# Scores of three pairs laid end to end in shared blocks, and four sequence-closing turns moved from TensorE to DMA

## The chip, the cores and the metric

The kernel runs on one core of one Trainium2 chip. The metric is the device time of one execution in microseconds (us), lower is better. Each run on record carries a state, and one that took over 1.5% longer than the fastest of its kernel is called slow. All runs compared here are in the fast state unless said otherwise. A "ratio" is the mean time of one kernel's fast runs over the mean of the fast runs of the kernel before in the same rounds, so it is not quite the ratio of the medians that are quoted.

## The reference, cut to what matters

Eight sequences of 576 tokens with 8 heads of 64 go through causal attention, with 16 "beacon" keys that every query may see. The result, 4608 tokens by 512, goes through two dense layers with a leaky ReLU between.

```python
k_all = np.concatenate([beacon_k, k], axis=2)          # 16 + 576 keys
scores = scale * np.matmul(q, k_all.transpose(0, 1, 3, 2))
scores = np.where(causal, -1000000000.0, scores)       # beacons are never masked
a = np.exp(scores - scores.max(-1, keepdims=True))
a /= a.sum(-1, keepdims=True) + 1e-09
x = np.matmul(a, v_all)                                # then 4608 x 512
h = x @ w_in                                           # 512 -> 2048
out = np.maximum(0.01 * h, h) @ w_out                  # 2048 -> 512
```

## The kernel before

Heads are worked in pairs: 4 pairs a sequence, 32 in all, numbered 0 to 31. The two heads of a pair stand on SBUF partitions 0 to 63 and 64 to 127, so the two score matmuls use the two halves of TensorE's rows at the same time: in the profile of before a block with 976 columns for each head takes 0.52 us, where 1952 columns one after the other would take 0.82 at the 0.216 us of a feed-forward matmul of 512. Keys are cut into 5 tiles; only queries that may see a tile are computed. Before the change, a pair's scores are four PSUM tiles, computed two at a time. I call the matmuls of scores that stand together in TensorE's order a **block**.

```python
SCORES = [
    [(0, 0, 512, 0)],                            # block 1: 512 + 464 columns
    [(1, 112, 464, 512)],
    [(2, 240, 336, 976), (0, 496, 80, 1312)],    # block 2: 336 + 80 + 208 + 80
    [(3, 368, 208, 1440), (4, 496, 80, 1648)],
]
...
for c, q0, w, col in parts:
    for par in range(2):                         # the two heads, 64 rows each
        ps_ = slice(par * 64, par * 64 + 64)
        nc.tensor.matmul(out=sc[:, par, col - c0 : col - c0 + w],
            lhsT=kT[ps_, c * 128 : (c + 1) * 128], rhs=qT[ps_, q0 : q0 + w], ...)
nc.scalar.activation(out=aT[:, :, c0 : c0 + w], in_=sc[:, :, 0:w], func=AF.Exp, scale=0.125)
```

After the values of a pair (`av`), its result `x_nat` must be turned into `xT` for the first dense layer. Three of four pairs of a sequence are turned by DMA (`x_turn`); the last one is turned on TensorE, because the feed-forward matmuls of that sequence are waiting for it. SP (SyncE) is the engine whose queue issues the DMA turns, the loads of V and the output stores.

```python
def finish(g):
    if g in xs:
        x_transposes(g)          # 5 matmuls on TensorE and a copy on VectorE
    ready[0] = chunks_with(g)    # from here on, groups of these 512 tokens may run
...
if old and (g - 2) % NPAIR < NPAIR - 1:
    x_turn(g - 2)                # two DMA transposes on SP's queue
```

Between the attention parts, TensorE's order is filled with feed-forward groups of four matmuls (`acc`): 16 groups of each layer for each 512 tokens. All orders are fixed by the program, engine by engine. (Two profiles of the changed kernel, after and r_after, show 69 instructions of GpSimd, from 103 to 126 and from 160 to 186 us, in the same order, though it stood idle before a copy of keys in one, 4.73 us, and before a copy of queries in the other, 6.20 us.)

## Time and profile before

| | before |
|---|---|
| time | 349.67 us median of 3 (349.06 to 349.69) |
| span in the profile | 347.5 us |
| TensorE busy | 336.1 us, 97% |
| GpSimd, ScalarE, VectorE busy | 57%, 54%, 26% |
| DMA, share of 16 engines, first two thirds / last quarter | 0.5 to 1.2 / about 0.1 |

The prediction below shows and reads the lines that matter: TensorE is the bound from about 60 us on (busy 19.65 to 19.89 of every 20 us until 340). What it says of SP's queue is about the DMA transposes; the added ones are the turns of pairs 19, 23, 27 and 31. Since TensorE's first 66 us are an opening with its own waits for loads, I use one more figure throughout: **the loop**, from the first instruction after the opening (the two second-layer groups behind the transposes of pair 9's keys) to the end of the last matmul. In the chain of before it is 65.81 to 343.56, which is 277.75 us.

### The profile page before, as it was taken

Reading aid. Unit: us, or ns where it says so; the run is one execution under the profiler, and the core shown is the slowest. Engines: PE = TensorE matmul, PEld = TensorE weight load, DVE = VectorE, ACT = ScalarE, POOL = GpSimd, SP = SyncE. Lnnn points to the kernel's source line nnn. Section 1 sums busy time; section 2 is a strip of 40 time slices with the busy share of each in tenths; the row PEclk is TensorE's granted clock in tenths of the full one; section 3 lists DMA queues with packets and bytes.
Section 4 is the critical chain, followed back from the end, with each engine's and each line's share of the span. In section 5 each row is a group of like instructions: output and inputs, shape, how many; then the busy total and the mean of one; then the engine's idle time right before and its main releaser. Section 6 shows DMA issues by size and latency. Waiting matters only on the chain.

```text
span 347.5 us, 7329 instructions
## 1 busy us (share of the span) xinstructions
PE 336.1 (97%) x2951; PEld 168.6 (49%) x2997; DVE 88.8 (26%) x215; ACT 187.9 (54%) x278; POOL 197.9 (57%) x364
## 2 busy tenths in 40 slices
PE   8998999999999999999999999999999999999995
PEld 7664465444444444544444444444454554444442
DVE  3383255103233113311222123212321231000111
ACT  4875864576535873488337843684368204633300
POOL 4794785489997699749974897679422000000000
PEclk9999999999999999999999999999999999999999
DMA  7989999999689747974796469646110120000021
GB/s 141 194 145 208 192 166 194 205 214 154 170 147 226 163 84 107 213 175 80 110 227 142 78 120 226 135 82 103 66 61 18 34 96 32 0 30 32 30 86 65
DMA packets 95857, 43.02 MB, mean 124 GB/s; under 512 B 79824, under 2 KB 90192, under 8 KB 95824
## 3 DMA queue, kind: packets, MB, share of 16 engines
q1 hardware_dynamic: 83200, 28.87, 37.6%
q0 software_dynamic: 12208, 13.49, 26.1%
q8 instruction: 23, 0.38, 0.5%
q10 hardware_dynamic: 416, 0.20, 0.2%
q14 instruction: 10, 0.08, 0.1%
HBM read 37.22 MB, written 9.44 MB: 134 GB/s over the span
## 4 chain that ended last, share of the span: by engine, by line
PE 86%; DMA 6%; DVE 2%; issue 2%; SPq 2%; ACT 1%; POOL 1%; ACTq 0%
PE acc L401 36%; PE acc L385 35%; PE sc L285 7%; PE av L337 7%; DMA w_in_sb<-in_moe_w_in_dram 3%; DMA v_raw<-in_v_dram 2%; SPq L199 1%; DMA v_raw<-in_k_dram 1%; ACT aT L294 1%; DVE x_nat L347 1%; PE tp L359 1%; PE tp L234 0%; DVE kT L246 0%; POOL aT L304 0%; PE tp L241 0%
## 5 line engine op out<-in xcount | busy, mean ns | idle before, releaser
L294 ACT ACTIVATE aT<-sc 128x1024 bf16<-128x1024 f32 (+3 forms) x128 | 104.8, 871 | 62.3 <-PE sc L285 58.7
L385 PE MATMUL acc<-xT,w_in_sb 128*128 128x512 bf16 x551 | 135.4, 379 | 2.4 <-DMA w_in_sb<-in_moe_w_in_dram 0.8
L401 PE MATMUL acc<-w_out_sb,gT 128*128 128x512 bf16 x555 | 134.5, 379 | 1.5 <-issue 0.6
L392 ACT ACTIVATE gT<-acc 128x512 bf16<-128x512 f32 x144 | 85.3, 604 | 76.2 <-PE acc L385 74.1
L304 POOL TENSOR_SCALAR_AFFINE_SELECT aT<-aT 128x256 bf16<-128x256 bf16 (+2 forms) x160 | 57.8, 390 | 49.7 <-ACT aT L294 46.9
L385 PEld LDWEIGHTS <-w_in_sb 128*128 128x128 bf16 x576 | 52.0, 98 | 62.8 <-issue 6.0
L401 PEld LDWEIGHTS <-gT 128*128 128x128 bf16 x576 | 52.0, 98 | 60.7 <-issue 4.8
L413 DVE COPY osb<-acc 128x512 f32<-128x512 f32 x35 | 24.2, 692 | 93.1 <-PE acc L401 87.7
L337 PEld LDWEIGHTS <-aT 128*128 128x128 bf16 (+1 forms) x960 | 37.2, 98 | 13.6 <-issue 1.1
L346 DVE RECIPROCAL rec<-av 128x6 f32<-128x6 f32 x64 | 11.9, 186 | 114.3 <-PE av L337 114.1
L337 PE MATMUL av<-v_aug,aT 128*128 128x65 bf16 (+1 forms) x960 | 40.3, 194 | 0.1
L285 PE MATMUL sc<-qT,kT 64*128 64x80 bf16 (+4 forms) x384 | 36.2, 283 | 1.7 <-DVE kT L246 0.8
L347 DVE TENSOR_TENSOR x_nat<-av,rec 128x384 bf16<-128x384 f32 x64 | 31.4, 491 | 2.2
L267 POOL COPY qT<-q_turn 128x576 bf16<-128x576 bf16 x22 | 26.2, 1189 | 9.0 <-PE av L337 4.5
L285 PEld LDWEIGHTS <-kT 64*128 64x128 bf16 x384 | 12.2, 94 | 27.4 <-issue 21.0
L267 POOL COPY kT<-k_turn 128x576 bf16<-128x576 bf16 x21 | 24.9, 1186 | 0.7 <-DMA k_turn<-k_nat 0.6
L214 POOL CAST v_aug<-v_raw 128x512 bf16<-128x512 f32 (+1 forms) x39 | 22.6, 613 | 2.4 <-DMA v_raw<-in_v_dram 2.4
L148 POOL DMA_DIRECT2D k_raw<-in_k_dram x31 | 19.1, 617 | 5.6 <-DMA w_out_sb<-in_moe_w_out_dram 5.6
L148 POOL DMA_DIRECT2D q_raw<-in_q_dram x32 | 19.7, 617 | 0.8 <-POOLq L661 0.8
L160 POOL COPY q_nat<-q_raw 128x1152 bf16<-128x1152 bf16 x12 | 13.7, 1141 | 1.8 <-DMA q_raw<-in_q_dram 1.8
L160 POOL COPY k_nat<-k_raw 128x1152 bf16<-128x1152 bf16 x12 | 13.7, 1144 | 0.0
L246 DVE COPY qT<-tp 128x576 bf16<-128x576 bf16 x10 | 7.6, 756 | 19.3 <-PE tp L241 13.3
(43 smaller groups left out, 76.9 us busy)
## 6 DMA issues: line engine op xcount, KB each, us to landing
out_dram<-osb SPq DMA_DIRECT2D x35, 256.0 KB, 2.5
v_raw<-in_v_dram SPq DMA_DIRECT2D x24, 256.0 KB, 6.6
q_raw<-in_q_dram POOLq DMA_DIRECT2D x32, 144.0 KB, 6.2
k_raw<-in_k_dram POOLq DMA_DIRECT2D x31, 144.0 KB, 6.2
w_in_sb<-in_moe_w_in_dram POOLq DMA_DIRECT2D x2, 1024.0 KB, 10.4
w_out_sb<-in_moe_w_out_dram POOLq DMA_DIRECT2D x2, 1024.0 KB, 11.1
v_raw<-in_v_dram SPq DMA_DIRECT2D x8, 224.0 KB, 3.2
v_raw<-in_v_dram SPq DMA_DIRECT2D x8, 160.0 KB, 7.3
```

Of the source, the lines that this page charges most:

```text
L148: loaded["qk", g, which] = nc.gpsimd.dma_start(out=raw_of(b, grp)[which][rows], in_=(q, k)[which][b, 2 * hp : 2 * hp + 2].rearrange("h (p ...
L160: copy(out=dst[rows], in_=src[rows].rearrange("p h i d -> p i h d"))
L267: copy(out=operand(g, which).rearrange("c (p i) -> c p i", i=RI), in_=turned[b, grp][which][:, :, e].rearrange("c i p -> c p i"),)
L285: nc.tensor.matmul(out=sc[:, par, col - c0 : col - c0 + w], lhsT=kT[ps_, c * 128 : (c + 1) * 128], rhs=qT[ps_, q0 : q0 + w], start=True, s ...
L294: nc.scalar.activation(out=aT[:, :, c0 : c0 + w], in_=sc[:, :, 0:w], func=AF.Exp, scale=0.125)
L304: nc.gpsimd.affine_select(out=view, in_=view, compare_op=ALU.is_ge, fill=0.0, base=128 - n if lo == 0 else 0, channel_multiplier=-1, patte ...
L337: nc.tensor.matmul(out=avv[:, n, 0 : D + 1], lhsT=aT[0 : ROWS[c], par, a0 : a0 + 128], rhs=va[0 : ROWS[c], c, 2 * hp + par, :], start=(c = ...
L347: nc.vector.tensor_tensor(out=x_nat[:, t0:t1].rearrange("p t e d -> p (t e) d"), in0=avv[:, :, 0:D], in1=rec[:, n0:n1, None].to_broadcast( ...
L385: nc.tensor.matmul(out=acc, lhsT=w_in_sb[:, j, fc * 128 : (fc + 1) * 128], rhs=xT[:, j, i * 512 : (i + 1) * 512], start=(j == 0), stop=(j ...
L392: nc.scalar.activation(out=gT[i][:, fc, :], in_=acc, func=AF.Prelu, alpha=0.01)
L401: nc.tensor.matmul(out=acc, lhsT=gT[i][:, fc, t * 128 : (t + 1) * 128], rhs=w_out_sb[:, fc, :], start=(fc == 0), stop=(fc == NF - 1),)
L413: nc.vector.tensor_copy(out=osb, in_=acc)
```

## The change

The intent is to take work out of TensorE's order. From pair 14 on, the scores of a pair are one strip of 1664 columns (576 + 464 + 336 + 208 + 80). Three strips are cut together into ten PSUM tiles of up to 512 columns, and the ten tiles are issued as five blocks of two, not six blocks of four pieces. The last pairs of sequences 4 to 7 (pairs 19, 23, 27 and 31) are turned by DMA like the others. Both need a new way to place the feed-forward groups: a list of timed events, with the groups spread evenly between the ends of sequences and three of them (`KEPT`) held back as cover behind each end. Loads of queries and keys move with the events.

```diff
+    LAID = 14
+    FLAT = [0, 576, 1040, 1376, 1584, 1664]
...
+    def stretch(parts):
+        sc = ps_sc.tile([128, 2, 512], FP32, name="sc", tag="sc")
+        at = 0
+        for g, lo, hi in parts:
+            for c in range(NKB):
+                a, b = max(lo, FLAT[c]), min(hi, FLAT[c + 1])
+                ...                              # one matmul a head for each piece
+        for g, lo, hi in parts:
+            nc.scalar.activation(out=probs[g][:, :, lo:hi], in_=sc[:, :, at : at + hi - lo], func=AF.Exp, scale=0.125)
+            ...                                  # and the masks of the finished tiles
...
-            if old and (g - 2) % NPAIR < NPAIR - 1:
-                x_turn(g - 2)
+        CUTS = [(0, 512, 1024, 1536, 1664), (0, 384, 896, 1376, 1664), (0, 224, 736, 1248, 1664)]
+        BLOCKS = [((0, 0),), ((0, 1),)], [((0, 2),), ((0, 3), (1, 0))], [((1, 1),), ((1, 2),)], [((1, 3), (2, 0)), ((2, 1),)], [((2, 2),), ((2, 3),)]
+        ONPE = (11, 15)
...
+            if g not in ONPE:
+                events.append((g + 2.63, 5, x_turn, (g,)))
+            if g >= LAID and (g - LAID) % 3 == 0:
+                for i in range(5):
+                    events.append((g + 0.01 + 0.6 * i, 2, block, (g, i)))
...
+                    events.append((4 * b + 1.1, 6, run, ("t%d.0" % (b + 1),)))   # turn of the next sequence's q and k
...
+        KEPT = 3
+            todo = 2 * NF * ready[0] - KEPT - d0
+            aim = d0 + todo * (at - ends[w]) / (ends[w + 1] - ends[w])
```

More of the change, by code (lines that the diff above doesn't have):

```diff
@@ L60, with acol @@
     NA, NK = 4, 8
-    def acol(c, q0):
+    LAID = 14
+    FLAT = [0, 576, 1040, 1376, 1584, 1664]
+    def acol(g, c, q0):
+        if g >= LAID:
+            return FLAT[c] + q0 - OFF[c]
         if c == 0:
@@ L302, in mask, with triangle @@
         for lo, n, rows in MASKS[part]:
-            view = aT[0:rows, :, lo : lo + n]
-            nc.gpsimd.affine_select(
-                out=view,
-                in_=view,
-                compare_op=ALU.is_ge,
-                fill=0.0,
-                base=128 - n if lo == 0 else 0,
-                channel_multiplier=-1,
-                pattern=[[0, 2], [1, n]],
-            )
+            triangle(aT, lo, n, rows)
+    def triangle(aT, lo, n, rows):
+        view = aT[0:rows, :, lo : lo + n]
+        nc.gpsimd.affine_select(
+            out=view,
+            in_=view,
+            compare_op=ALU.is_ge,
+            fill=0.0,
+            base=128 - n if lo == 0 else 0,
+            channel_multiplier=-1,
+            pattern=[[0, 2], [1, n]],
+        )
+    def stretch(parts):
+        sc = ps_sc.tile([128, 2, 512], FP32, name="sc", tag="sc")
+        at = 0
+        for g, lo, hi in parts:
+            qT, kT = qk[g]
+            for c in range(NKB):
+                a, b = max(lo, FLAT[c]), min(hi, FLAT[c + 1])
+                if a >= b:
+                    continue
+                q0 = OFF[c] + a - FLAT[c]
+                for par in range(2):
+                    ps_ = slice(par * 64, par * 64 + 64)
+                    nc.tensor.matmul(
+                        out=sc[:, par, at : at + b - a],
+                        lhsT=kT[ps_, c * 128 : (c + 1) * 128],
+                        rhs=qT[ps_, q0 : q0 + b - a],
+                        start=True,
+                        stop=True,
+                        skip_group_check=True,
+                    )
+                at += b - a
+        at = 0
+        for g, lo, hi in parts:
+            if lo == 0:
+                probs[g] = a_bufs[g % NA]
+            nc.scalar.activation(
+                out=probs[g][:, :, lo:hi], in_=sc[:, :, at : at + hi - lo], func=AF.Exp, scale=0.125
+            )
+            at += hi - lo
+            for c in range(NKB):
+                n = (112, 128, 128, 128, 80)[c]
+                if lo < FLAT[c] + n <= hi:
+                    triangle(probs[g], FLAT[c], n, ROWS[c])
     xs, avs = {}, {}
@@ L335, in value @@
                 for c in range(t + 1):
-                    a0 = acol(c, q0)
+                    a0 = acol(g, c, q0)
                     nc.tensor.matmul(
@@ L492, in run @@
                 cast_v(a[0], a[1], a[1] + 1)
+            elif op == "a":
+                cast_v(a[0], a[1], a[1] + 1, act)
             elif op == "C":
@@ L573, in loads @@
         def loads(g, late):
-            b, hp = divmod(g, NPAIR)
             if g in (8, 12) and late:
                 parts.extend((g // 4 + 1, c) for c in range(NKB))
-            if g in EXTRA:
-                run(EXTRA[g][late])
-                return
-            if not late:
-                if has(g + 1):
-                    in_order(g + 1)
-                return
-            if b == B - 1:
-                return
-            if hp == 0:
-                parts.extend((b + 1, c) for c in range(NKB))
-            if hp < 2:
-                for n in range(2):
-                    run("l%d.0 l%d.1" % ((4 * b + 4 + 2 * hp + n,) * 2))
-            else:
-                run("t%d.%d" % (b + 1, hp - 2))
-            if hp == 3:
-                cast_v(b + 1)
+            run(EXTRA[g][late])
         EXTRA = {
@@ L601 @@
             12: ("r13", "l16.0 l16.1 l17.0 l17.1"),
-            13: ("r14", "l18.0 l18.1 l19.0 l19.1"),
+            13: ("r14", ""),
         }
-        for g in range(8, NG + 3):
-            if has(g):
-                loads(g, 0)
-            chunks = chunks_with(g - 3) if g - 3 >= 2 * NPAIR else ready[0]
-            groups = 2 * NF * chunks - done1[0] - done2[0]
-            steps = NPAIR - (g - 2) % NPAIR if g > 2 * NPAIR + 5 else 2 * NPAIR + 6 - g
-            n = -(-(groups - 2) // steps)
-            slots = [0] * 8
-            for i in range(n):
-                slots[(2, 5, 1, 6, 0, 4, 3, 7)[i % 8]] += 1
-            owed = [0]
-            def slot(n):
-                owed[0] += slots[n]
-                if parts and n % 2 == 0:
-                    load_v_part(*parts.pop(0))
-                while owed[0] and fill():
-                    owed[0] -= 1
-            old = g - 2 >= 2 * NPAIR and has(g - 2)
-            if has(g):
-                run("s%d.0 m%d.0 s%d.1" % (g, g, g))
-            slot(0)
-            if g - 3 >= 2 * NPAIR:
-                finish(g - 3)
-            slot(1)
-            if old:
-                value(g - 2, 0)
-            slot(2)
-            slot(3)
-            if has(g):
-                run("s%d.2 m%d.1 s%d.3 m%d.2" % (g, g, g, g))
-                loads(g, 1)
-            slot(4)
-            if old:
-                value(g - 2, 1)
-            if old and (g - 2) % NPAIR < NPAIR - 1:
-                x_turn(g - 2)
-            for n in (5, 6, 7):
-                slot(n)
@@ new lines, with block @@
+        CUTS = [(0, 512, 1024, 1536, 1664), (0, 384, 896, 1376, 1664), (0, 224, 736, 1248, 1664)]
+        BLOCKS = [((0, 0),), ((0, 1),)], [((0, 2),), ((0, 3), (1, 0))], [((1, 1),), ((1, 2),)], [((1, 3), (2, 0)), ((2, 1),)], [((2, 2),), ((2, 3),)]
+        FIRST = 2 * NPAIR
+        ONPE = (11, 15)
+        def block(g0, i):
+            for tile in BLOCKS[i]:
+                stretch([(g0 + r, CUTS[r][n], CUTS[r][n + 1]) for r, n in tile])
+        events = []
+        for g in range(FIRST, NG):
+            if g < LAID:
+                events.append((g, 0, loads, (g, 0)))
+                events.append((g + 0.02, 1, run, ("s%d.0 m%d.0 s%d.1" % (g, g, g),)))
+                events.append((g + 0.5, 1, run, ("s%d.2 m%d.1 s%d.3 m%d.2" % (g, g, g, g),)))
+                events.append((g + 0.52, 1, loads, (g, 1)))
+            if g > LAID:
+                events.append((g - 1.35, 0, in_order, (g,)))
+            events.append((g + 2.25, 3, value, (g, 0)))
+            events.append((g + 2.62, 4, value, (g, 1)))
+            if g not in ONPE:
[3 more added lines that the diff above has]
+                    events.append((g + 0.01 + 0.6 * i, 2, block, (g, i)))
@@ new lines @@
+        ends = [FIRST]
+        for g in range(FIRST, NG):
+            at = g + 3.1 if g // NPAIR * NPAIR + NPAIR - 1 in ONPE else g + 3.5
+            events.append((at, 2, finish, (g,)))
+            if g % NPAIR == NPAIR - 1:
+                ends.append(at)
+        for b in range(2, B - 1):
+            at = 8.6 if b == 2 else 12.6 if b == 3 else 4 * b + 1.75
+            for n in range(NKB):
+                events.append((at + 0.24 * n, 6, load_v_part, (b + 1, n)))
+            if b > 2:
+                l = "l%d.0 l%d.1 "
+                if b > 3:
+                    events.append((4 * b + 0.52, 6, run, ((l + l) % ((4 * b + 4,) * 2 + (4 * b + 5,) * 2),)))
+                    events.append((4 * b + 1.1, 6, run, ("t%d.0" % (b + 1),)))
+                    events.append((4 * b + 2.0, 6, run, ((l + l) % ((4 * b + 6,) * 2 + (4 * b + 7,) * 2),)))
+                else:
+                    events.append((13.8, 6, run, ("t4.0 l18.0 l18.1 l19.0 l19.1",)))
+                events.append((4 * b + 2.8, 6, run, ("t%d.1" % (b + 1),)))
+                events.append((4 * b + 3.9, 6, cast_v, (b + 1,)))
@@ L645 @@
+        events.sort(key=lambda e: e[:2])
+        KEPT = 3
+        w, d0 = 0, done1[0] + done2[0]
+        for at, _, what, args in events:
+            while w + 2 < len(ends) and at > ends[w + 1]:
+                w, d0 = w + 1, done1[0] + done2[0]
+            todo = 2 * NF * ready[0] - KEPT - d0
+            aim = d0 + todo * (at - ends[w]) / (ends[w + 1] - ends[w])
+            while done1[0] + done2[0] < aim and fill():
+                pass
+            what(*args)
         while done2[0] < NCH * NF:
```

## The prediction

> **What bounds the kernel now.** I read the busy table and the chain that ended last first, then the chain in order of time for one pair in the middle, then the waits of the score line, and last the stretch where the attention work ends.
>
> ```profile
> PE 336.1 (97%) x2951; PEld 168.6 (49%) x2997; DVE 88.8 (26%) x215; ACT 187.9 (54%) x278; POOL 197.9 (57%) x364
> ...
> PE 86%; DMA 6%; DVE 2%; issue 2%; SPq 2%; ACT 1%; POOL 1%; ACTq 0%
> ```
>
> TensorE is busy for 97% and carries 86% of the chain; the other 14% lies mostly in the first 29 us (loads). In the table by stretches of 20 us, PE is busy 19.65 to 19.89 of 20 from 60 us to 340 us. So from about 60 us on the time is the sum of what stands in TensorE's order, and a microsecond taken out of that order is a microsecond off the end, as long as nothing new makes TensorE wait. The chain, for a bit more than one pair:
>
> ```profile
> 173.48 1.73 PE acc L401 x8
> 175.21 0.41 PE sc L285 x8
> 175.62 0.97 PE acc L401 x4
> 176.58 0.56 PE av L337 x18
> 177.14 0.06 issue
> 177.20 2.54 PE acc L401 x11
> 179.73 0.52 PE sc L285 x4
> 180.25 0.97 PE acc L401 x4
> 181.22 0.26 PE tp L359 x5
> 181.48 0.87 PE acc L401 x4
> 182.34 0.37 PE av L337 x12
> ```
>
> Columns are start, duration, what. Four feed-forward matmuls take 0.86 us (8 take 1.73) where nothing disturbs them, but 0.97 after a score block. A block of scores costs more than its columns: the 4-matmul block streams 512 + 464 = 976 columns; the two heads run side by side on 64 rows each, so at 2.4 columns per ns (my reading of 512 columns in 0.216 us) that is 0.41 us, yet it takes 0.52, and 0.11 more is lost in the matmuls behind it. The 8-matmul block streams 336 + 80 + 208 + 80 = 704 columns, 0.29 us, and takes 0.41 plus the same 0.11. So **every score block carries about 0.225 us that does not depend on its size**. The waits of that line agree:
>
> ```profile
> L285 PEld LDWEIGHTS <-kT x384: 92/94/97, 7.2 to 265.9; 64*128 64x128 bf16 x192
> ...
> issue: 21.0, 50
> ```
>
> The weight loads ahead of 50 blocks sat 0.42 us each with nothing they waited for[...].
>
> Third, the end of the attention part, where the last pair is turned on TensorE:
>
> ```profile
> 283.38 4.28 PE acc L401 x19
> 287.65 0.02 issue
> 287.68 0.32 DVE osb L413
> 288.00 0.29 issue
> 288.29 0.46 DVE xT L364
> 288.74 0.04 issue
> 288.79 4.91 PE acc L385 x22
> ```
>
> There the chain leaves TensorE: the copy of the transposed block stands behind an output copy on VectorE. The list of TensorE's waits puts only 0.24 us of idle on it, since three matmuls that don't need the copy run meanwhile.
>
> [...] Scores use 64-row tiles, everything else 128 rows, so each block is one change and one change back. [...] This bears on the new pieces of 16 and 48 columns. The trace of before has none that short, but its 80-column pieces show no floor above 33 ns for a pair of heads (the 8-matmul block would otherwise show more than the fixed 0.225). [...] The trace has all of them on SP's queue, in order with output stores and loads of V; that is what could delay the added ones.
>
> **The change part by part.** The order of instructions of both builds was compared.
>
> *Fewer blocks.* Pairs 14 to 31 are 18 pairs: 2 blocks each before, 36; 5 blocks for 3 pairs after, 30. Six blocks fewer x 0.225 = 1.35 us off TensorE.
>
> *Fewer columns.* A pair was 976 + 704 = 1680 columns, now 1664 (the 16 recomputed ones of the first key tile go): 18 x 16 / 2400 = 0.12 us off.
>
> *More, shorter matmuls.* Three pairs are now cut into 23 pieces, not 18; with two heads and 6 triples that is 60 matmuls more. Columns are the same, so only a floor costs: with at most 33 ns for a pair of heads, a 16-column piece (7 ns of columns) costs up to 26 ns more, a 48-column one (20 ns) up to 13, a 64-column one (27 ns) up to 6. That is 45 ns a triple, up to 0.27 us in all; I take 0.2 added.
>
> *Last pairs turned by DMA.* Pairs 19, 23, 27 and 31 lose 5 transposes each: 4 x 0.26 = 1.04 us off TensorE, and four copies of 0.45 us off VectorE, beside the path. The order shows just this: 60 matmuls more, 20 fewer. The wait of 0.24 and its 0.05 of issue at 288 us go too: 0.3 off.
>
> *ScalarE.* The forms of the exponential give its cost:
>
> ```profile
> L294 ACT ACTIVATE aT<-sc 128x1024 bf16<-128x1024 f32 x32 | 32.7, 1022 | 39.2 <-PE sc L285 35.9 <-POOL kT L267 3.2
> ...
> L294 ACT ACTIVATE aT<-sc 128x576 bf16<-128x576 f32 x32 | 21.0, 656 | 0.5 <-PE sc L285 0.3
> ```
>
> That is (1022 - 656) / 448 = 0.82 ns an element and 185 ns fixed. Three pairs are still 12 activations, because the two tiles that cross from one pair to the next need two; 9984 elements against 10080. So 10.38 us a triple against 10.46: nothing.
>
> *Even spreading of feed-forward groups.* It moves work and takes none out: 262 groups of 0.8625 us remain after the common start, in both.
>
> As a check I added up the order of before from its first loop block (65.81 us): 262 groups x 0.8625 = 226.0; 24 pairs x (0.63 + 0.52) = 27.6; values of 24 pairs x 0.93 = 22.3; 6 turns x 0.26 = 1.6; sum 277.4. The trace has 277.75 (to 343.56). So the sum misses 0.35 us, of which 0.3 is the wait above.
>
> Sum: -1.35 - 0.12 - 1.04 - 0.3 + 0.2 = -2.6 us; 349.67 becomes 347.0, 0.75% less.
>
> **The rivals.** *The DMA turn arrives late.* For pair 30 in before, the last value matmul ends at 275.5, VectorE ends at 276.16, and SP issues the two turns:
>
> ```profile
> 276.19 1.20 SPq L370 DMA_TRANSPOSE xT<-x_nat  x1
> 277.44 1.23 SPq L374 DMA_TRANSPOSE xT<-x_nat  x1
> ```
>
> With 2.5 us median from issue to landing it is in place at 279.9, 4.4 us after the value. In the new order 8 groups (32 matmuls, 6.9 us) stand between the last value of pair 31 and the first matmul that reads its turn; at pairs 19, 23 and 27 it is 8 to 9 us, in part other work. So it is hidden by 2.5 us or more, unless SP's queue is held up: the longest landing in before is 7.9 us, and at pairs 19 and 23 the turns of queries and keys of a later sequence stand ahead in the queue. If all four came late by 1 us, the DMA part would gain nothing and the result is 348 to 348.5.
>
> *GpSimd becomes the bound.* Loads of queries and keys now come 0.6 to 0.8 of a pair (5 to 7 us) ahead of the copies that need them, and take 6.2 us to land after four issues of 0.62. GpSimd runs in order, so it will stand idle 2 to 3 us twice a sequence. Per sequence it has masks 7.2, ordering of queries and keys 10.4, casts 3, permutes 4.6 and issues 4.9, in all 30 us, of some 36. With 5 us of idle it is at 35: it fits, just. Masks are done 13 us or more before the values that read them, which absorbs a lag. For it: 20.00 of 20 us busy in 80 to 100 us, without a wait of TensorE there. If it loses, 1 to 4 us come on top, 347.5 to 350.
>
> *ScalarE falls behind in runs of first-layer groups.* Each needs 0.60 of 0.86 us, and blocks of two full tiles now need 2.0 us at once every 5.4 us. Together that is about 93 to 95% of such a stretch, where before had about 92% (blocks of 1.97 and 1.52 us). One accumulator buffer more or less decides; I expect at most some tenths.
>
> *The fixed cost is per matmul and not per block.* Then 60 more matmuls would add and the merge would gain nothing: 348.4. Against it: blocks of 4 and of 8 matmuls show the same excess.
>
> **Range and chances.** The sums are of repeated durations with a check to 0.35 us in 278, so downward there is little: 346. Upward the stalls above give 348.5. Runs of one kernel scatter by 0.6 us (349.06 to 349.69). To be faster by 2% the gain would have to be 7 us, nearly three times the sum of all parts; slower by 2% would need a stall of 9.6 us, more than GpSimd's rival makes.
>
> **What would show it.** Right: idle of score weight loads ahead of 44 blocks and not 50 or so in the same 0.42 us each; score blocks of 0.54 us for 1024 columns; 50 transposes of the values' results and not 70; no idle of TensorE on the turned tile; TensorE's last matmul at 340.9 or so, not 343.56. Wrong: new idle of TensorE released by a DMA into the turned tile, by GpSimd's keys or masks, or by an activation freeing a score or accumulator buffer; or blocks with 12 matmuls clearly longer than those with 6.

## The result, and the profile after

The changed kernel takes **348.02 us** (median of 6 runs, 347.17 to 349.42), beside 349.65 us for before (6 runs, 349.06 to 349.69). The ratio is 0.9957, with a 95% interval of 0.9935 to 0.9979. That is a gain of about 1.5 us: inside the predicted range, 1 us above the predicted 347.0. The interval lies wholly below 1, so the gain is clear of noise, but it is small, 0.4%.

The page of the profile after has these lines for the busy time and the chain that ended last:

```profile
PE 333.5 (96%) x2992; PEld 170.1 (49%) x3037; DVE 88.3 (26%) x211; ACT 187.5 (54%) x278; POOL 197.4 (57%) x364
...
PE 85%; DMA 6%; DVE 2%; SPq 2%; issue 2%; ACT 2%; POOL 1%; ACTq 0%
```

TensorE is still the bound and has 2.6 us less to do. The chain in order of time shows the new blocks (start, duration, what):

```profile
134.50 0.54 PE sc L334 x6
135.04 1.83 PE acc L443 x8
136.87 0.37 PE av L379 x12
137.24 2.59 PE acc L443 x12
139.83 0.57 PE sc L334 x12
140.40 0.66 PE av L379 x18
```

A block of 6 matmuls and one of 12 both stream 1024 columns for each head, which is 0.43 us at the 0.216 us that a feed-forward matmul of 512 columns takes. They take 0.54 and 0.57 us. The fixed part of 0.11 us going in is there again, and the 0.11 coming out now lies on whatever follows: 18 value matmuls take 0.66 us right behind a block and 0.56 elsewhere. The block with the 16- and 48-column pieces is only 0.03 us longer. A change from one kind of 128-row matmul to another showed nothing of this kind: behind the values at 136.87, 12 feed-forward matmuls take 2.59 us, 0.216 each.

At the end of the attention part, the same view of after:

```profile
282.34 2.54 PE acc L443 x11
284.88 0.86 PE acc L427 x4
285.74 0.86 PE acc L443 x4
...
288.33 4.75 PE acc L427 x22
```

The chain no longer leaves TensorE for the copy of the turned block. The loop goes from 66.78 to 341.88, which is **275.10 us: 2.65 us less than before, where 2.6 were predicted**. But the opening, whose instructions are the same in both, ended 0.97 us later, and the stretch behind the last matmul was 0.38 us longer (4.32 against 3.94 us). So this one profile gains only 1.3 us of span. The question for the experiments was whether the missing microsecond is chance in the opening, or something that the change causes.

### The profile page after: what moved, and what is told of

It reads as the page before. It is cut to its first block, busy times and chain, and to the rows that moved or that the text cites. A ratio compares the mean times of both kernels' runs of the same rounds, so it can differ in the third digit from the quotient of the medians.

```text
span 346.2 us, 7423 instructions
## 1 busy us (share of the span) xinstructions
PE 333.5 (96%) x2992; PEld 170.1 (49%) x3037; DVE 88.3 (26%) x211; ACT 187.5 (54%) x278; POOL 197.4 (57%) x364
## 4 chain that ended last, share of the span: by engine, by line
PE 85%; DMA 6%; DVE 2%; SPq 2%; issue 2%; ACT 2%; POOL 1%; ACTq 0%
PE acc L443 36%; PE acc L427 34%; PE av L379 7%; PE sc L334 5%; DMA w_in_sb<-in_moe_w_in_dram 3%; PE sc L290 2%; DMA v_raw<-in_v_dram 2%; SPq L204 1%; DMA v_raw<-in_k_dram 1%; ACT aT L299 1%; DVE x_nat L389 1%; ACT aT L347 0%; PE tp L239 0%; DVE kT L251 0%; POOL aT L312 0%
## 5 line engine op out<-in xcount | busy, mean ns | idle before, releaser
L443 PEld LDWEIGHTS <-gT 128*128 128x128 bf16 x576 | 53.0, 98 | 60.9 <-issue 2.7
L427 PEld LDWEIGHTS <-w_in_sb 128*128 128x128 bf16 x576 | 52.7, 98 | 61.4 <-issue 3.1
L312 POOL TENSOR_SCALAR_AFFINE_SELECT aT<-aT 128x256 bf16<-128x256 bf16 (+2 forms) x160 | 57.5, 391 | 43.8 <-ACT aT L347 29.3
L379 PEld LDWEIGHTS <-aT 128*128 128x128 bf16 (+1 forms) x960 | 36.4, 98 | 14.2 <-issue 4.1
L290 PE MATMUL sc<-qT,kT 64*128 64x512 bf16 (+3 forms) x168 | 17.0, 284 | 1.9 <-DVE kT L251 1.0
L334 PE MATMUL sc<-qT,kT 64*128 64x80 bf16 (+16 forms) x276 | 18.2, 255 | 0.1
L334 PEld LDWEIGHTS <-kT 64*128 64x128 bf16 x276 | 9.2, 94 | 14.1 <-issue 11.4
```

What stands on the lines that cost most here:

```text
L312: nc.gpsimd.affine_select(out=view, in_=view, compare_op=ALU.is_ge, fill=0.0, base=128 - n if lo == 0 else 0, channel_multiplier=-1, patte ...
L334: nc.tensor.matmul(out=sc[:, par, at : at + b - a], lhsT=kT[ps_, c * 128 : (c + 1) * 128], rhs=qT[ps_, q0 : q0 + b - a], start=True, stop= ...
L379: nc.tensor.matmul(out=avv[:, n, 0 : D + 1], lhsT=aT[0 : ROWS[c], par, a0 : a0 + 128], rhs=va[0 : ROWS[c], c, 2 * hp + par, :], start=(c = ...
L427: nc.tensor.matmul(out=acc, lhsT=w_in_sb[:, j, fc * 128 : (fc + 1) * 128], rhs=xT[:, j, i * 512 : (i + 1) * 512], start=(j == 0), stop=(j ...
L443: nc.tensor.matmul(out=acc, lhsT=gT[i][:, fc, t * 128 : (t + 1) * 128], rhs=w_out_sb[:, fc, :], start=(fc == 0), stop=(fc == NF - 1),)
```

## The experiments

Runs were made in three calls, each on one chip with its own runs of before. The first two (chip 4) are told first.

| run | what it has | loop in its profile, us | mean of fast runs, us (before) | ratio |
|---|---|---|---|---|
| r_before | before again | 277.75 | one run, state unknown | |
| r_after | the change again | 276.93 | 348.25 (349.82) | 0.9955 |
| e_blocks | blocks alone | 276.13 | 348.63 (349.82) | 0.9968 |
| e_turn | DMA turns alone | 279.04 | 352.91 (349.82) | 1.0098 |
| e_spread | neither, only the spreading | 277.34 | 349.61 (349.69) | 0.9996 |
| e_single | a block per tile | 281.47 | 353.72 (349.69) | 1.0114 |
| e_short | short pieces added | 277.60 | 349.87 (349.69) | 1.0006 |
| e_bare | turns not covered | 304.39 | 376.25 (349.69) | 1.0758 |

One run of e_blocks and one of e_short fell in the slow state and are left out of the means. All results were correct.

### r_before and r_after: the same two kernels again

> The kernel before, unchanged, for a second profile. Theory (the loop from pair 8 on gained 2.65 us: 277.75 us in the first profile of before, 275.10 us in that of after; the 1 us lost again lies in the opening loads, which landed later by chance): the loop takes 277.7 us again within 0.2, and its start may lie anywhere from 65.8 to 67 us. Rival (the longer program itself delays the opening[...]): the loop of this kernel starts at 65.8 us again within 0.15.

> The changed kernel, unchanged, for a second profile and more times. Theory: the loop takes 275.1 us again within 0.2, its start moves by some tenths from the 66.78 us of the first profile, and the times scatter over 1 us or more with a median near 347.5 to 348. Rival (program causes the late opening): the start is 66.8 us again within 0.15. Second rival (the scatter of 347.2 to 349.4 comes from waits inside the loop, which come and go): the loop differs from 275.1 by over 0.5 us.

The loop of before took 277.75 us again, to the hundredth. Its start moved from 65.81 to 66.36 us, and that of the changed kernel from 66.78 to 66.38. So the starts move by half a us in both kernels, and the late opening of the first profile was chance as far as two profiles of each can tell. But the loop of the changed kernel took 276.93 us and not 275.10, which is the second rival. The timeline of TensorE names the difference; these are the only two instructions of the loop with idle time before them (the bracket has the idle us and what ended it):

```profile
124.32 0.49 PE L334 MATMUL sc<-qT,kT 64*128 64x224 bf16 x6 [0.80 <-POOL kT L272]
184.07 0.39 PE L427 MATMUL acc<-xT,w_in_sb 128*128 128x512 bf16 x1 [0.68 <-DMA xT<-x_nat]
```

The first waits for the keys of pair 16, which GpSimd orders only after their DMA turn has landed. GpSimd itself stood idle for 6.2 us before it: the turn of these queries took 9.6 us from issue to landing, where the median of the run is 3.4, and that of the keys took 3.63 us to issue. So this wait too goes back to a late transfer. The second waits for the turn of pair 19, one of the four moved to DMA. SP's queue and the chain of r_after around it:

```profile
174.33 1.33 SPq L260 DMA_TRANSPOSE k_turn<-k_nat  x1
...
176.38 2.56 SPq L412 DMA_TRANSPOSE xT<-x_nat  x1
179.00 1.23 SPq L416 DMA_TRANSPOSE xT<-x_nat  x1
```

```profile
179.00 5.03 DMA xT<-x_nat
```

The first turn took 2.56 us to issue where 1.2 is usual, and the second took 5.03 us from issue to landing where the median of before was 2.5. The last value matmul of pair 19 ended at 174.50, so the turn needed 9.5 us and not the 4.4 us that the prediction read off pair 30. (VectorE had the block ready at 175.18. SP issued its turn 1.2 us later, behind the key turn and an output store.) The first profile came close to the same wait: there this turn landed at 182.06, 8.1 us after the value and some 0.7 us before the matmul that reads it. Pair 30 of before is at 276 us, where the share of DMA is about 0.1; in r_after it is 0.74 from 160 to 180 us and 0.98 from 180 to 200 us, with stores, loads of V and loads of queries and keys beside it.

This wait and the one on keys come and go. In the first profile neither was there. The times scatter as well: the 15 runs of the changed kernel have a standard deviation of 1.08 us, the 36 of before 0.60. That the late turns make this scatter isn't shown: e_blocks below, without the four DMA turns, has 0.90, and e_short, with them, 0.55. The execution of the second profile took 349.40 us, above the mean of 348.25. Taking both waits away leaves 276.93 - 0.80 - 0.68 = 275.45 us.

### e_blocks, e_turn and e_spread: the parts alone

```diff
 e_blocks
-        ONPE = (11, 15)
+        ONPE = (11, 15, 19, 23, 27, 31)
 e_turn
-    LAID = 14
+    LAID = B * NPAIR          # no laid strips; the loads of pairs 8 to 13 as in the change
 e_spread: both edits
```

> Only the merged blocks (and the even spreading); the last pairs of the four sequences stay on TensorE. Theory (0.225 us for each of six blocks, 0.12 for columns, 0.2 back for short pieces): the loop takes 277.75 - 1.3 = 276.45 us, and the time is 0.3 to 0.4% under before. Rival (the fixed cost is per matmul, so merging gains nothing): the loop takes 277.6 to 277.9 us. Rival (the merge gains all and the DMA turn nothing): 275.1 us.

> Only the DMA turns of the four last pairs (and the even spreading); scores stay in two blocks a pair throughout. Theory: the loop takes 277.75 - 1.04 - 0.3 = 276.4 us, and no idle of TensorE on the turned tile. Rival (turns arrive late and give it back): 277 us or more with such idle.

> Neither part: two blocks a pair, last pairs turned on TensorE, only the even spreading of feed-forward groups and the moved loads. Theory (spreading moves work and takes none out): the loop takes 277.5 us within 0.3, and the time is that of before within 0.15%. Rival (the spreading itself gains or loses, by fewer or more waits): over 0.5 us off.

**e_spread** is as before in time (0.9996, interval 0.9985 to 1.0007). Its loop is 0.41 us shorter, and there is no idle of TensorE in it: the 0.3 us at the last turn of before went by the spreading alone, although that turn is still on TensorE here.

**e_blocks** has a loop of 276.13 us, 1.21 less than e_spread; 1.27 was worked out (-1.35 - 0.12 + 0.2). The rival by which the fixed cost belongs to matmuls and not to blocks is out.

**e_turn** is 3.1 us slower on the mean than before, and its loop of 279.04 us, with idle on the turned tile, is what the rival said. The profile shows where:

```profile
183.87 0.39 PE L427 MATMUL acc<-xT,w_in_sb 128*128 128x512 bf16 x1 [0.83 <-DMA xT<-x_nat]
221.49 0.39 PE L427 MATMUL acc<-xT,w_in_sb 128*128 128x512 bf16 x1 [1.55 <-DMA xT<-x_nat]
```

These are the turns of pairs 19 and 23, and the landing of the latter took 5.64 us from issue. Before that it had stood in SP's queue, as the prediction feared: VectorE had its block ready at 210.98, and SP issued the turn at 214.52, behind the key turn of a later sequence (211.89, 1.91 us to issue) and a store. Without the 2.4 us of idle the loop is 276.7 us, near the expected 276.4. So the work taken out is right, and the rival "turns arrive late and give it back" is what happened: without the merged blocks the four turns cost more than they save (why they come later there isn't shown beyond this). In the timed runs it lost more than in its profile (median 353.32 against 351.41 for the profiled execution); the waits of those runs weren't seen.

From e_blocks to the first profile of the changed kernel the loop falls by 1.03 us: the four turns save exactly their 1.04 us when none of them comes late. On the mean of the timed runs the turns add only 348.63 - 348.25 = 0.4 us of gain, and the intervals of the two ratios (0.9954 to 0.9983 and 0.9936 to 0.9974) overlap, so that even this isn't clear of noise. The gain that is shown in time is that of the blocks.

### e_single: what a block costs

```diff
-                for i in range(5):
-                    events.append((g + 0.01 + 0.6 * i, 2, block, (g, i)))
+                for i in range(10):
+                    events.append((g + 0.01 + 0.3 * i, 2, block, (g, i)))
 ...
-            for tile in BLOCKS[i]:
+            for tile in BLOCKS[i // 2][i % 2 : i % 2 + 1]:
```

> The changed kernel with each score tile as a block of its own: ten blocks for three pairs in place of five, the same matmuls and columns. Theory (0.225 us per block, for the change to 64 rows and back): 6 x 5 = 30 blocks more, minus those that fall next to each other with no group between, so +6 us in the loop, 281 us in all. Rival (the cost is per matmul or per column): no change, 275.1 us.

The order has exactly 30 blocks more (97 against 67), and the loop is 281.47 us, 6.37 more than the 275.10 of the changed kernel. There is no idle in it. So a block costs 6.37 / 30 = **0.212 us**, with the same matmuls and columns. What TensorE does in that time isn't shown. The ratios of the timed runs (1.0114 and 0.9955) give 5.6 us or 0.19 us a block, and their intervals include 0.212. In the chain, a block of 512 columns (0.216 us) takes 0.32, and the four matmuls behind it 0.97 in place of 0.86:

```profile
153.59 0.32 PE sc L334 x4
153.91 0.97 PE acc L427 x4
```

### e_short: what a short piece costs

```diff
+                for u, w in ((0, 16), (16, b - a - 16)):
                     for par in range(2):
-                        out=sc[:, par, at : at + b - a], ... rhs=qT[ps_, q0 : q0 + b - a],
+                        out=sc[:, par, at + u : at + u + w], ... rhs=qT[ps_, q0 + u : q0 + u + w],
```

> The changed kernel with the first 16 columns of each of the pieces in a matmul of their own (22 of the 23 pieces of a triple are cut): 6 x 22 = 132 pairs of heads more, the same columns and the same blocks. Theory (a floor of at most 33 ns for a pair of heads; 7 ns of it are columns that stood there before): up to +132 x 0.026 = 3.4 us in the loop, 278.5 us. [...] Rival (no floor): 275.1 us.

The loop is 277.60 us without idle, 2.50 more, so one more pair of 16-column matmuls costs 2.50 / 132 = 19 ns beyond its columns, and 26 ns in all with the 7 ns of columns. That lies under the bound of 33 ns taken from 80-column pieces. The ratios of the timed runs (1.0006 and 0.9955) give a smaller 13 ns beyond the columns. In the change itself this makes about 19 ns for the piece of 16 columns and 6 for that of 48 in each triple, 0.15 us in six triples; 0.2 was predicted.

### e_bare: a turn without cover

```diff
-            at = g + 3.1 if ... in ONPE else g + 3.5
+            at = g + 3.1 if ... in ONPE else g + 2.65
-        KEPT = 3
+        KEPT = 0
```

> The changed kernel with the first-layer groups of a new sequence right behind the last values of a sequence, no groups kept between: the four DMA turns are bare. Theory (a turn is in place 4.4 us after the last value matmul, and 6.9 to 9 us of other work hid it): TensorE waits about 4.4 us four times, +17.6 us, 365 us in all, 15 to 20 us allowed for the queue ahead of the turns. Rival (the landing is much faster than the median from issue tells): under +8 us.

TensorE waits for all four turns, as its timeline shows:

```profile
186.69 2.31 PE L427 MATMUL acc<-xT,w_in_sb 128*128 128x512 bf16 x5 [4.85 <-DMA xT<-x_nat]
233.21 3.57 PE L427 MATMUL acc<-xT,w_in_sb 128*128 128x512 bf16 x9 [8.12 <-DMA xT<-x_nat]
274.39 5.19 PE L427 MATMUL acc<-xT,w_in_sb 128*128 128x512 bf16 x17 [3.69 <-DMA xT<-x_nat]
312.86 15.91 PE L427 MATMUL acc<-xT,w_in_sb 128*128 128x512 bf16 x61 [3.71 <-DMA xT<-x_nat]
```

At pairs 27 and 31, where no loads run any more, a turn costs 3.7 us; at pairs 19 and 23 it costs 4.9 and 8.1. The prediction's 4.4 us held for the quiet end of the kernel alone. The waits sum to 20.4 us, just over the 15 to 20 allowed, but the loop is 29.3 us longer. Of the other 9 us, about 8 are the clock, by an estimate: in stretches of 0.1 and 0.2 us the granted clock is 0.50 from 185.0 to 191.8, 229.4 to 236.2, 273.8 to 277.2 and 311.3 to 318.1 us, and 16.2 us of this is work behind the four waits that would take half as long at full clock (the block of 10 score matmuls at 189.01 takes 0.97 us, the same kind of block at 285.47, at clock 1.00, 0.55). The table by stretches shows it after the first wait (stretch, us, busy times, and in the column before the last two the granted clock):

```profile
185.00:187.00 2.00, 0.31 (x1) 0.13 (x2) 0.00 (x0) 0.00 (x0) 0.00 (x0) 0.50 0.12 25
...
189.00:191.00 2.00, 2.00 (x14) 0.87 (x14) 0.00 (x0) 1.95 (x4) 0.63 (x2) 0.50 1.34 221
...
193.00:195.00 2.00, 2.00 (x21) 1.15 (x20) 0.75 (x2) 1.10 (x3) 1.46 (x3) 1.00 0.85 111
```

After an idle stretch of 4.9 us TensorE ran at half its clock for some 5 us. The granted clock was 0.50 after each of the four waits, and 1.00 again within 2.8 to 5.3 us of work. The half clock began 3.2, 4.3, 3.0 and 2.2 us after TensorE's last matmul; what sets these times isn't shown. The shortest of the four, 3.7 us, brought it too. Behind waits of up to 2.33 us in r_after, e_turn and f_queue the matmuls ran at full speed (four took 0.86 us at 184.46 in r_after and at 221.88 in e_turn, eight took 1.89 at 225.86 in f_queue). So in e_bare the long waits cost more than themselves: 20.4 us of idle, and about 8 us of slower work by the estimate above.

### f_kept, f_turn_kept, f_early and f_queue: attempts to keep the gain

The last four runs (chip 7, before 349.85 us on the mean of 43 runs, standard deviation 0.86) tried to take the waits away.

```diff
 f_kept, f_early; f_turn_kept on top of e_turn
-        KEPT = 3
+        KEPT = 8
 f_early, besides
-                    events.append((13.8, 6, run, ("t4.0 l18.0 l18.1 l19.0 l19.1",)))
+                    events.append((13.54, 6, run, ("t4.0",)))
+                    events.append((13.8, 6, run, ("l18.0 l18.1 l19.0 l19.1",)))
 f_queue
-                    events.append((4 * b + 1.1, 6, run, ("t%d.0" % (b + 1),)))
+                    events.append((4 * b + 1.66, 6, run, ("t%d.0" % (b + 1),)))
```

> The changed kernel with 8 feed-forward groups kept behind a sequence's end in place of 3: 5 x 0.8625 = 4.3 us more of other work between the last values and the first matmul that reads the turned tile; nothing else changes. Theory (the gain was given back by turns of pairs 19 and 23 that land late, 0.7 us in the second profile of the changed kernel): no idle of TensorE on the turned tile, loop 275.1 us but for a wait on keys at pair 16 (0.8 us) that may come or not, median 347.2, scatter (standard deviation) falling from 1.1 toward 0.6 us. Rival (the scatter has nothing to do with the turn): mean and scatter as those of the changed kernel, 348.2 and 1.1.

> The kernel with DMA turns alone, which was 3.1 us slower than before on the mean, with 8 groups kept in place of 3. Theory (its whole loss is late turns at pairs 19 and 23, 2.4 us of idle in its profile, and what follows from them): the loop takes 276.4 us and the time is 1.3 us under before. Rival (the loss lies elsewhere, in GpSimd or in the queue of DMA): still over before.

> As f_kept, and the queries and keys of pairs 16 and 17 are permuted and sent to their DMA turn before GpSimd orders pair 15, some 2.5 us earlier. Theory (the wait on keys at pair 16 is the other source of scatter): no idle of TensorE in the loop, 275.1 us, mean 0.2 to 0.5 us under that of f_kept. Rival (that wait hardly ever shows): equal to f_kept within 0.2 us.

> The changed kernel, 3 groups kept, but the next queries and keys are permuted and turned only after the turn of the sequence's last pair has been put on SP's queue (pairs 19 and 23). If the turn is late because query and key turns stand ahead of it in that queue: it is issued 1 to 2 us earlier and lands in time, mean 347.5. If it is late because its landing takes 5 us among loads and stores, wherever it stands: a wait of some tenths stays in some executions, mean and scatter as in the changed kernel.

| run | mean of fast runs, us | standard deviation, us | ratio |
|---|---|---|---|
| f_kept | 349.57 | 0.65 | 0.9991 |
| f_turn_kept | 351.13 | 0.76 | 1.0042 |
| f_early | 350.17 | 0.83 | 1.0014 |
| f_queue | 351.49 | 1.22 | 1.0050 |

None of them is as fast as the changed kernel (0.9955 against its own runs of before, on chip 4; it wasn't run on chip 7), so my expectation of their times fell. In **f_kept** the wait on the turn is indeed gone, and the scatter is 0.65. But 8 groups are held back in every stretch, also in the first one, so TensorE comes to the scores of pairs 9 to 11 sooner than GpSimd has their queries and keys. The timeline of TensorE in f_kept:

```profile
79.08 0.58 PE L290 MATMUL sc<-qT,kT 64*128 64x512 bf16 x4 [0.19 <-POOL kT L272]
...
86.50 0.59 PE L290 MATMUL sc<-qT,kT 64*128 64x512 bf16 x4 [0.96 <-POOL qT L272]
```

With a third such wait of 0.24 us this is 1.4 us of idle, and the loop takes 276.9 us; 275.5 without it. In this profile the opening too ended later, at 67.9 us. **f_early** has the same three waits and one more of 0.33 us, so moving pair 16 forward showed no gain: its mean is 0.6 us above that of f_kept, where a gain or no change was expected, though the intervals overlap. **f_turn_kept** halves the loss of e_turn (ratio 1.0042 against 1.0098), with the same three waits and 0.75 us left on the turn of pair 23. So late turns are part of its loss; the rest is only in part accounted for, by 1.4 us of the three waits in its profile.

In **f_queue**, TensorE waits 2.33 us in one place, at 225.86, not for a turn but for an accumulator. The chain leads to an output store:

```profile
217.84 7.18 DMA out_dram<-osb
...
225.11 0.70 DVE osb L455
```

A store that takes 2.4 us in the median took 7.2 among loads and turns, VectorE waited for the output buffer (there are two), and the accumulator stayed full. So it isn't only the place in the queue: DMA's share is 1.1 to 1.3 from 217 to 225 us, and with the turns moved another transfer came late there. But this profile is of the fastest of the 14 executions (349.73 us), so what makes the mean 1.6 us slower than before, which neither alternative had, wasn't seen. Their mean granted clock, 0.9951 beside 0.9981 for before, allows about 1 us of it at most (an estimate: 0.003 of 350 us).

What stays open: how much of the 1.1 us between the loop's gain (2.65) and the mean gain of the timed runs (349.82 - 348.25 = 1.57) is the turn, how much the keys and how much something that no profile caught. The clock has hardly a part in it: the mean granted clock is 0.9974 in the 15 runs of the changed kernel and 0.9976 in the 36 of before, a difference worth under 0.1 us by an estimate (0.0002 of 349 us). A version that holds 8 groups only from pair 15 on, which would leave the first stretch as it was, wasn't run. No run beat the changed kernel.

## Why the prediction was right

By its own steps:

- **Fewer blocks** (-1.35 us at 0.225 each): right. e_single measured 0.212 us a block with nothing else changed, which makes 1.27 for six. The sign to look for, idle weight loads ahead of 44 blocks of scores, came out as 40 (27 + 13, 16.7 us in all, 0.42 each), beside 50 before. (The prediction's 512 columns in 0.216 us are 2.37 columns per ns, not 2.4; this moves the cost of a block by 0.01 us at most.)
- **Fewer columns and more short matmuls** (-0.12 and +0.2): right together with the blocks, since e_blocks lies 1.21 us under e_spread where 1.27 was summed. e_short puts a pair of short matmuls at 26 ns, where at most 33 was assumed.
- **Last pairs by DMA** (-1.04): right in size for the work, 1.03 us of loop between e_blocks and the first profile of the changed kernel. As time it did not come: 0.4 us on the mean.
- **The wait at 288 us** (-0.3): gone, but put down to the wrong part. e_spread, which keeps that turn on TensorE, lost it too (loop -0.41), so "moves work and takes none out" was 0.4 us off for the spreading.
- **ScalarE**: right, no wait of TensorE in the loop was for an activation.
- **Rival, the DMA turn arrives late**: this is where the missing microsecond lies, in part at least, and where a term was mis-sized. "It is in place 4.4 us after the value" was read off pair 30 of before, which turns in a quiet stretch; beside loads and stores the first profile shows 8.1 and r_after 9.5 us at pair 19. The prediction named the place (pairs 19 and 23, with turns of a later sequence ahead in the queue) and the cost if late (348 to 348.5, where the mean of the timed runs, 348.25, lies), but took the cover of 8 to 9 us as enough.
- **Rival, GpSimd becomes the bound**: it did not, but a wait on its keys came in one of two profiles (0.80 us at pair 16). The slack was worked out for the masks, on which no wait of TensorE was seen, and not for the queries and keys, whose turns landed up to 9.6 us after issue.

So the sum of the work was met within 0.05 us in a profile without waits; that it came so close is in part luck, since the 0.3 us of the wait was put down to the wrong part. TensorE's last matmul ended at 341.88 and 343.31 us in the two profiles, not at 340.9. The time came out 1 us over: in r_after because the cover of one DMA turn and of one pair's keys was sized by quiet transfers, in the other executions probably for the same reason, which isn't shown.

## What to carry to other kernels

Where TensorE is the bound, count how often it changes between 64-row and 128-row matmuls: each excursion cost about 0.21 us here, in blocks of 512 to 1024 columns, so longer and fewer blocks paid (1.21 us of loop in e_blocks), and a piece of 16 columns inside a block cost only 19 ns beyond its columns. Before a transfer takes the place of work on the critical engine, size its cover by the slowest landing in the stretch where it will run, not by the median of the whole kernel: landings that TensorE waited for took 5.0 us in r_after and 5.6 in e_turn, beside a median of 2.5 in before. And look at the scatter: a second profile of the same kernel showed waits (0.80 and 0.68 us) that the first did not have.
